# Transposing one batch entry's states ahead of the tokens and the other three behind the first probabilities

## The chip, the cores and the metric

One core of a Trainium2 chip runs the whole kernel. The metric is the device time of one execution in microseconds (us). The kernel before took 754.21 us (median of 3 runs, 754.07 to 754.38). The trace is of one further execution, the profiled one. Its engines: PE (TensorE), ACT (ScalarE), DVE (VectorE), POOL (GpSimd), SP (which here only issues DMAs).

## The reference, cut to what matters

```python
B, H, S, Ns, D = 4, 8, 512, 32, 64
scores  = x @ state.T / sqrt(D);  a  = softmax(scores)     # x reads the states
xread   = a @ state
scores2 = state @ x.T / sqrt(D);  a2 = softmax(scores2)    # the states read x
sread   = a2 @ x
t = concat([xread, sread], axis=2)          # (B, H, S + Ns, D) -> 2176 tokens x 512
t = elu(t @ w_in)   @ w_out                 # 512 -> 2048 -> 512, f64 weights in DRAM
t = mish(t @ w2_in) @ w2_out
```

## The kernel before, in words

Everything is float32; a product that needs full accuracy is split into high and low parts (three matmuls). The 16 slices of 128 hidden columns are one loop ("steps"); first-layer steps run over the four batch entries, second-layer steps over five blocks of tokens.

The part around the change is the head. For batch entry b and half hf of the heads, `token_reads` loads x (`xb`), turns it (`xT`, two turns of four 128x128 transposes, each evacuated by one copy), multiplies by the states (`scores`, 16 matmuls per half), takes the maximum over the 32 states (`mx`, L614), subtracts it (L615), exponentiates (L617), sums, inverts and multiplies (L621 to L624), turns the probabilities (`pT`, L629) and copies them to `x1` (L633). A copy of the raw scores (L618) goes to SBUF and then to DRAM (`s2d`), for the reads in the other direction much later. The states are kept as block-diagonal tiles `sd[b]`: `states()` loads all of them (`st_raw`, two DMAs on the ACT queue), transposes them in three groups of 2, 2 and 4 (entry 0; entry 1; entries 2 and 3; L388) and copies each half of `sd[b]` out of PSUM (8 copies, L394, shown under the helper's line L275). `xread @ w_in` is not formed: `fold` multiplies the states into the first weight (`m`, L516), so that the first step's matmul `h` (L721) is `m` against `x1`.

Weights come as 64-bit floats: each 512 KB tile is a DMA on the SP queue, one ACT conversion (`wy`, L439) and three DVE operations (L448, L450, L461 or L467).

The order of all instructions is computed at build time by `Plan`. Each operation has an engine (or `EITHER` of ACT and DVE), a cost and a due time, derived backwards from its successors or given. `run` (L117) repeatedly picks, over all engines, the operation with the smallest key

```python
k = (t, due, seq)      # t: the earliest start, by the planner's own clock
```

so the due time decides only between operations that could start at the same planned moment; an engine that is free takes whatever can start first. Buffers and PSUM banks are waited for as well. Early banks are dealt out in the fixed cycle of L342 in the order in which operations are added: in the kernel before entry 0's states and the second turn of half 1's x have the same bank, acc0. Afterwards every engine runs its own list strictly in that order, and semaphores guard what is read. Constants: raw-score copies are due at `T[index[1, b, 0]] - 8.0`, with `T` = 20.0 for the first step; x loads are due at -30, the warm-up turns at -40.

Of the kernel before, what the change touches and what calls it, by code (L numbers as in the profile page):

```python
# [22 lines left out]
P = 128  # L23
# [192 lines left out]
def attention_elu_mish(  # L216
# [49 lines left out]
    def buf(pool, tag, bufs, shape, dt=F32, name=None):  # L266
        return Buf(pool, tag, bufs, shape, dt, f"{name or tag}{next(serial)}")
# [103 lines left out]
        attention.append(op)  # L371
        return op

    def states():

        raw = buf("w", "w_out", NF, [P, 2 * B, 2, D], F32, "st_raw")
        for i in range(2):
            A(ACTQ, 128.0, lambda i=i: nc.scalar.dma_start(
                out=raw[:, :, i, :], in_=state.rearrange("b (g h) n d -> (h n) (b g) d", g=2)),
              w=[(raw, i)], due=-50.0)  # L380
        for b in range(B):
            A("POOL", 0.5, lambda b=b: nc.gpsimd.memset(sd[b], 0.0), w=[("sd", b, i) for i in range(2)], due=-50.0 + b)
        for b0, b1 in ((0, 1), (1, 2), (2, 4)):
            pt = bank("st")

            def turn(b0=b0, b1=b1, pt=pt):
                for i in range(2 * (b1 - b0)):
                    nc.tensor.transpose(pt[:, i * P:(i + 1) * P], raw[:, 2 * b0 + i].rearrange("p t d -> p (t d)"), ident)  # L388

            A("PE", 0.25 * (b1 - b0), turn, r=["ident", (raw, 0), (raw, 1)], w=[pt])  # L390
            for b in range(b0, b1):
                for i in range(2):
                    r = slice(i * D, (i + 1) * D)
                    A(EITHER, {"ACT": 0.41, "DVE": 0.43}, lambda e, b=b, b0=b0, i=i, r=r, pt=pt: copy(  # L394
                        e, sd[b][r, :, :, i, :],
                        pt[r, (b - b0) * 2 * P:(b - b0 + 1) * 2 * P].rearrange("p (g h n) -> p g h n", g=2, n=NS)),
                        r=[pt], w=[("sd", b, i)])
# [166 lines left out]
    def token_reads(b, hf):  # L564
        xb = load_x(b, hf, X_DUE if early else None)
        if b not in x1:
            if b:
                x1[b] = buf("work", "x", 2, [P, 2, 2, S], F32R, f"x1_{b}_")
            else:
                x1[b] = buf("w", "w_out", NF, [P, 2, S], F32, f"x1_{b}_")  # L570
        xt = x1[b]
        if early and hf:
            xT = buf("w", "w_out", NF, [P, 2, S], F32, "xT")
            prr = buf("w", "w_out", NF, [P, 2, NC, P], F32, "prob")
            pr, raw = (lambda: prr[:, 0]), (lambda: prr[:, 1])
            kp, kr = (prr, 0), (prr, 1)
            held = [prr]
        else:
            xT = buf("at", "xT", 1, [P, 2, S], F32)
            kp, kr = buf("at", "prob", 1, [P, NC, P], F32), buf("at", "raw", 1, [P, NC, P], F32)  # L580
            pr, raw = (lambda: kp.t), (lambda: kr.t)
            held = [kp, kr]
        mx = buf("at", "mx", 2, [P, NC * HH])
        sm = buf("at", "sm", 2, [P, NC * HH])
        held += [mx, sm]
        lag = 0.0 if early else 1.0
        ahead = TOKENS_AHEAD[b]
        for q in range(2):
            pt = bank("xT")

            def turn(q=q, pt=pt):
                for i in range(4):
                    nc.tensor.transpose(  # L593
                        pt[:, i * P:(i + 1) * P],
                        xb[:, 2 * q + i // 2, i % 2 * 2:i % 2 * 2 + 2, :].rearrange("p c d -> p (c d)"), ident)

            A("PE", NC * 0.11, turn, r=["ident", (xb, q)], w=[pt], lag=lag, place=[xT])
            A(EITHER, both(S), lambda e, q=q, pt=pt: copy(e, xT[:, q, :], pt.t), r=[pt], w=[(xT, q)])
        pt = bank("scores")
        for q in range(2):  # L600
            def score(q=q):
                for i in range(4):
                    h, c = 2 * q + i // 2, i % 2 * 2
                    nc.tensor.matmul(  # L604
                        pt.t.rearrange("p (c h n) -> p c h n", c=NC, n=NS)[:, c:c + 2, h, :],
                        lhsT=xT[:, q, i * P:(i + 1) * P], rhs=sd[b][:, hf, h, :, :], start=True, stop=True)

            A("PE", 0.9, score, r=[(xT, q), ("sd", b, 0), ("sd", b, 1)], w=[(pt, q)], lag=lag, place=held)
        all_c = [(pt, q) for q in range(2)]
        G = NC * HH  # L610
        prg = lambda: pr().rearrange("p c (h n) -> p (c h) n", n=NS)
        pv = lambda: pt.t.rearrange("p (g n) -> p g n", n=NS)
        wide = lambda t: t.t.unsqueeze(2).to_broadcast([P, G, NS])
        A("DVE", 0.69, lambda: nc.vector.tensor_reduce(mx.t, pv(), AX.X, ALU.max), r=all_c, w=[mx])  # L614
        A("DVE", 0.69, lambda: nc.vector.tensor_tensor(prg(), pv(), wide(mx), ALU.subtract),  # L615
          r=all_c + [mx], w=[kp])
        A("ACT", 0.64, lambda: nc.scalar.activation(pr(), pr(), AF.Exp, scale=SCALE), r=[kp], w=[kp], lag=lag)  # L617
        A(EITHER, both(S), lambda e: copy(e, raw().rearrange("p c f -> p (c f)"), pt.t), r=all_c, w=[kr],  # L618
          due=T[index[1, b, 0]] - 8.0)
        A(SP, 256.0, lambda: nc.sync.dma_start(out=s2d[:, b, hf], in_=raw()), r=[kr], w=[("s2d", b, hf)])  # L620
        A("DVE", 0.69, lambda: nc.vector.tensor_reduce(sm.t, prg(), AX.X, ALU.add), r=[kp], w=[sm])  # L621
        A("DVE", 0.17, lambda: nc.vector.tensor_scalar(sm.t, sm.t, EPS, None, ALU.add), r=[sm], w=[sm])
        A("DVE", 0.25, lambda: nc.vector.reciprocal(sm.t, sm.t), r=[sm], w=[sm])
        A("DVE", 0.69, lambda: nc.vector.tensor_tensor(prg(), prg(), wide(sm), ALU.mult), r=[kp, sm], w=[kp])  # L624
        p2 = bank("pT")

        def turn2():
            for c in range(NC):
                nc.tensor.transpose(p2[:, c * P:(c + 1) * P], pr()[:, c, :], ident)  # L629

        A("PE", NC * 0.11, turn2, r=["ident", kp], w=[p2], lag=lag, place=[xt])
        if not b:
            A(EITHER, both(S), lambda e: copy(e, xt[:, hf, :], p2.t), r=[p2], w=[(xt, hf)], lag=ahead)  # L633
        else:
            A(EITHER, both(S), lambda e: copy(e, xt[:, 0, hf, :], p2.t), r=[p2], w=[(xt, hf, 0)])
            A("DVE", 0.69, lambda: nc.vector.tensor_tensor(
                xt[:, 1, hf, :], p2.t, xt[:, 0, hf, :].bitcast(F32), ALU.subtract),
              r=[p2, (xt, hf, 0)], w=[(xt, hf)], lag=ahead)
# [184 lines left out]
    def retire(kind, blk, j, acc, s):  # L823
# [20 lines left out]
        t0, n = (NC * blk, NC) if kind == 1 else BLOCKS2[blk]  # L844
        second = kind == 1 and j == NF - 1 and (blk, 0, NF) not in FIRST
        for i, a in enumerate(acc):
            rows = x2d[:, i, t0 * P:t0 * P + S] if kind == 1 else None
            names = [("x2d", t0 + c, i) for c in range(NC)]
            if second:
                o = buf("work", "wraw", 3, [P, DM], F32, f"half{blk}_{i}_")  # L850
                add(SP, 256.0, lambda o=o, rows=rows: nc.sync.dma_start(out=o.t, in_=rows), r=names, w=[o], lag=2.0)
                add("DVE", 0.69, lambda o=o, a=a: nc.vector.tensor_tensor(o.t, a.t, o.t, ALU.add),
                    r=[a, o], w=[o], due=due + 0.7 * i)
            else:
                o = place(f"o{kind}_{blk}_{i}_")
                add(EITHER, both(S), lambda e, o=o, a=a: copy(e, o.t, a.t), r=[a], w=[o], due=due + 0.7 * i)
            if kind == 1:
                add(SP, 256.0, lambda o=o, rows=rows: nc.sync.dma_start(out=rows, in_=o.t), r=[o], w=names,
                    due=due + 4.0)
            elif t0 + i < NT - 1:  # L860
                b, c = divmod(t0 + i, NC)
                to = out[b * ST:b * ST + S, :].rearrange("(p c) e -> p c e", c=NC)[:, c, :]
                add(SP, 256.0, lambda o=o, to=to: nc.sync.dma_start(out=to, in_=o.t), r=[o], due=due + 4.0)
            else:
                add(SP, 256.0, lambda o=o: nc.sync.dma_start(
                    out=out.rearrange("(b s) e -> b s e", b=B)[:, S:, :], in_=o.t), r=[o], due=due + 4.0)
# [16 lines left out]


    warm()
    states()
    token_reads(0, 0)
    token_reads(0, 1)
    early = False
    s_state = index[0, 0, 0]  # L890
    for j in range(NF):
# [75 lines left out]
GATE_READS, GATE_READS_STEP, GATE_SECOND = 10, 4, 14  # L967
BACKLOG, RATE = 3.0, 330.0
OBUFS = 4
WHOLE_OUT = 6  # L970
X_WEIGHT = 1.5
POOL_LO = set()
# [28 lines left out]
```

## Time and profile before

| what | value |
| --- | --- |
| median of 3 runs | 754.21 us |
| the profiled execution's own time | 754.74 us |
| its span, first to last instruction | 752.8 us |
| PE busy | 732.8 us, 97% |
| DVE busy | 556.5 us, 74% |
| ACT busy | 423.3 us, 56% |
| mean DMA rate | 109 GB/s, 81.7 MB |

The span leaves 1.9 us around it in the profiled execution, which is 0.53 us longer than the median of the runs. Busy time is summed over instructions; PE's pipelined matmuls overlap a little.

### The profile page before, as it was taken

The page shows a single profiled execution, that of the slowest core. Times are in us where ns is not written, and L with a number is a line of the kernel's source. Part 1 is how long each engine was busy: PE and PEld are TensorE (multiplying, and loading weights), DVE is VectorE, ACT ScalarE, POOL GpSimd, SP SyncE. Part 2 cuts the span into 40 slices and gives each one's busy share as a digit, 9 for nine tenths or more (in the row PEclk, how much of TensorE's full clock was granted, in tenths as well). Part 3 has the DMA queues.
Part 4 walks back from the last instruction along what each step waited for, and adds up shares of the span by engine and source line. Part 5 has one row for each costly group of instructions (what it writes and reads, how often), then busy time and mean ns, then how long its engine had stood idle before and what let it go on. Part 6 is the DMA issues. An engine that isn't in the chain of part 4 may idle for free.

```text
span 752.8 us, 11041 instructions
## 1 busy us (share of the span) xinstructions
PE 732.8 (97%) x4098; PEld 597.8 (79%) x4098; DVE 556.5 (74%) x1047; ACT 423.3 (56%) x757; POOL 10.6 (1%) x27
## 2 busy tenths in 40 slices
PE   5899999999999999999999999999999999999995
PEld 5346677788787879878888888888889898989894
DVE  6989899988689895698998856565566666666653
ACT  3584767655566663487666545454455555455542
POOL 1000000010000000000000000000000000000000
PEclk9899999999999999999999999999999999999998
DMA  9954667363585643565855103000020020001001
GB/s 227 293 148 105 165 156 224 112 168 112 152 250 175 192 139 100 183 199 181 281 175 187 40 1 98 0 1 1 0 99 1 1 84 1 1 1 42 1 1 42
DMA packets 66872, 81.71 MB, mean 109 GB/s; under 512 B 22660, under 2 KB 45188, under 8 KB 66820
## 3 DMA queue, kind: packets, MB, share of 16 engines
q1 hardware_dynamic: 64740, 80.49, 36.0%
q10 hardware_dynamic: 2080, 0.52, 0.3%
q8 instruction: 32, 0.52, 0.3%
q14 instruction: 20, 0.16, 0.1%
HBM read 59.51 MB, written 21.50 MB: 108 GB/s over the span
## 4 chain that ended last, share of the span: by engine, by line
PE 94%; DMA 3%; DVE 1%; ACT 1%; issue 0%; SPq 0%; ACTq 0%
PE acc_acc L815 16%; PE acc_acc L817 15%; PE acc_acc L816 15%; PE h L735 12%; PE h L737 12%; PE h L736 12%; PE fold L516 2%; PE acc_acc L803 2%; PE h L711 2%; PE h L721 2%; DMA raw_in<-in_moe_w_in 2%; PE scores L604 1%; DMA xb<-in_x 1%; PE pT L629 1%; PE sr L663 1%; PE xT L593 1%
## 5 line engine op out<-in xcount | busy, mean ns | idle before, releaser
L754 ACT ACTIVATE e<-h 128x512 f32<-128x512 f32 (+1 forms) x148 | 83.1, 562 | 117.5 <-PE h L737 104.9
L779 ACT CAST g<-e 128x512 fp32r<-128x512 f32 (+1 forms) x142 | 82.4, 580 | 60.8 <-PE acc_acc L817 24.3
L737 PE MATMUL h<-x,w_in 128*128 128x384 f32 (+1 forms) x320 | 114.6, 358 | 0.0
L735 PE MATMUL h<-x,w_in 128*128 128x384 f32 (+1 forms) x320 | 114.4, 358 | 0.0
L736 PE MATMUL h<-x,w_in 128*128 128x384 f32 (+1 forms) x320 | 114.3, 357 | 0.0
L780 DVE TENSOR_TENSOR g<-e,g 128x512 fp32r<-128x512 f32 (+1 forms) x142 | 91.1, 642 | 22.3 <-ACT g L779 21.5
L817 PE MATMUL acc_acc<-w_out,g 128*128 128x512 f32 x272 | 106.9, 393 | 0.0
L816 PE MATMUL acc_acc<-w_out,g 128*128 128x512 f32 x272 | 106.7, 392 | 0.0
L815 PE MATMUL acc_acc<-w_out,g 128*128 128x512 f32 x272 | 105.9, 389 | 0.4 <-ACT g L779 0.4
L815 PE MATMUL acc_acc<-g,w_out 128*128 128x512 f32 x232 | 93.3, 402 | 0.0
L776 DVE TENSOR_TENSOR u<-u,e 128x384 f32<-128x384 f32 (+1 forms) x80 | 48.8, 610 | 57.8 <-ACT e L775 57.7
L817 PE MATMUL acc_acc<-g,w_out 128*128 128x512 f32 x232 | 90.5, 390 | 0.0
L816 PE MATMUL acc_acc<-g,w_out 128*128 128x512 f32 x232 | 90.5, 390 | 0.0
L774 ACT ACTIVATE e<-u,two 128x384 f32<-128x384 f32 (+1 forms) x80 | 52.8, 660 | 50.0 <-DVE u L772 49.8
L771 DVE TENSOR_SCALAR e<-e 128x384 f32<-128x384 f32 (+1 forms) x80 | 30.9, 387 | 48.2 <-ACT e L754 48.2
L735 PEld LDWEIGHTS h<-x,w_in 128*128 128x128 f32 x320 | 60.1, 188 | 7.2
L736 PEld LDWEIGHTS h<-x,w_in 128*128 128x128 f32 x320 | 60.1, 188 | 7.1
L737 PEld LDWEIGHTS h<-x,w_in 128*128 128x128 f32 x320 | 60.0, 188 | 4.9
L817 PEld LDWEIGHTS acc_acc<-w_out,g 128*128 128x128 f32 x272 | 51.0, 188 | 11.0 <-DVE g L780 0.3
L815 PEld LDWEIGHTS acc_acc<-w_out,g 128*128 128x128 f32 x272 | 51.1, 188 | 10.1 <-ACT g L779 0.9
L816 PEld LDWEIGHTS acc_acc<-w_out,g 128*128 128x128 f32 x272 | 51.0, 188 | 9.6
L815 PEld LDWEIGHTS acc_acc<-g,w_out 128*128 128x128 f32 x232 | 43.5, 188 | 13.5 <-issue 3.3
(126 smaller groups left out, 1168.9 us busy)
## 6 DMA issues: line engine op xcount, KB each, us to landing
raw_out<-in_moe_w_out SPq DMA_DIRECT2D x32, 512.0 KB, 3.9
raw_in<-in_moe_w_in SPq DMA_DIRECT2D x32, 256.0 KB, 5.9
raw_in<-in_moe_w_in SPq DMA_DIRECT2D x16, 512.0 KB, 4.3
w2d<-wv SPq DMA_DIRECT2D x32, 256.0 KB, 3.1
out<-o SPq DMA_DIRECT2D x17, 256.0 KB, 2.3
xb<-in_x SPq DMA_DIRECT2D x16, 256.0 KB, 4.6
x2d<-o SPq DMA_DIRECT2D x16, 256.0 KB, 2.6
xb<-in_x SPq DMA_DIRECT2D x32, 128.0 KB, 3.6
```

The costliest lines, as they stand in the source:

```text
L735: nc.tensor.matmul(h[:, :n], lhsT=wh, rhs=xh, start=(k == 0), stop=False)
L736: nc.tensor.matmul(h[:, :n], lhsT=wh, rhs=xl, start=False, stop=False)
L737: nc.tensor.matmul(h[:, :n], lhsT=wl, rhs=xh, start=False, stop=(k == nk - 1))
L754: add("ACT", act(n), lambda: nc.scalar.activation(E(), Hh(), AF.Exp), r=[h], w=[e])
L771: add("DVE", 0.1 + 0.00065 * n, lambda: nc.vector.tensor_scalar(E(), E(), E20, None, ALU.min), r=[e], w=[e])
L774: add("ACT", act(n) + 0.12, lambda: nc.scalar.activation(E(), U(), AF.Ln, bias=two), r=[u, "two"], w=[e])
L776: add("DVE", dve(n), lambda: nc.vector.tensor_tensor(U(), U(), E(), ALU.mult), r=[u, e], w=[u])
L779: add("ACT", act(n) + 0.01, lambda: nc.scalar.copy(g[:, 0, :n], E()), r=[e], w=[(g, 0)])
L780: add("DVE", dve(n), lambda: nc.vector.tensor_tensor(g[:, 1, :n], E(), g[:, 0, :n].bitcast(F32), ALU.subtract), r=[e, (g, 0)], w=[(g, 1)])
L815: nc.tensor.matmul(acc.t, lhsT=st[:, 0, :], rhs=mv[:, 0, :], start=fst, stop=False)
L816: nc.tensor.matmul(acc.t, lhsT=st[:, 0, :], rhs=mv[:, 1, :], start=False, stop=False)
L817: nc.tensor.matmul(acc.t, lhsT=st[:, 1, :], rhs=mv[:, 0, :], start=False, stop=lst)
```

## The change

Entry 0's transposes get a due time of -10. The other three entries' are added after both halves of entry 0's token reads and must come after the last copy of the probabilities to `x1` (`late_after`). The planner's cost of an early x turn goes from 0.44 to 0.84. Early copies of raw scores are due at 20 + 15 instead of 20 - 8. Because the operations are added in another order, early banks are dealt out differently: in the order entry 0's states, entry 0's x and scores, then the other states (att, acc1).

```diff
-    def states():
+    late_after, st_raw = [], []
+    def load_states():
         raw = buf("w", "w_out", NF, [P, 2 * B, 2, D], F32, "st_raw")
...
-        for b0, b1 in ((0, 1), (1, 2), (2, 4)):
+    def states(b0, b1):
...
-            A("PE", 0.25 * (b1 - b0), turn, r=["ident", (raw, 0), (raw, 1)], w=[pt])
+            op = A("PE", 0.25 * (b1 - b0), turn, r=["ident", (raw, 0), (raw, 1)], w=[pt], due=-10.0 if b0 == 0 and LATE else None,
+                   after=late_after if b0 and LATE else ())
...
-            A("PE", NC * 0.11, turn, r=["ident", (xb, q)], w=[pt], lag=lag, place=[xT])
+            A("PE", NC * (0.21 if early and LATE else 0.11), turn, r=["ident", (xb, q)], w=[pt], lag=lag, place=[xT])
...
-          due=T[index[1, b, 0]] - 8.0)
+          due=T[index[1, b, 0]] + (15.0 if early and LATE else -8.0))
...
-    states()
+    load_states()
+    states(0, 1)
+    if not LATE:
+        states(1, 2)
+        states(2, 4)
     token_reads(0, 0)
     token_reads(0, 1)
+    if LATE:
+        late_after.append(plan.writer[x1[0], 1])
+        states(1, 2)
+        states(2, 4)
...
+TILES_FROM = 4
+SPLIT_END = False
+LATE = True
```

The diff also adds two branches that these constants leave unused: scores by tiles for entries from `TILES_FROM` = 4 on (there are four, 0 to 3), and a last store in halves (`SPLIT_END` is False).

## Rows read from the trace of the kernel before

**Rows 1.** The page: the span, and two lines of the table of 40 equal slices (18.8 us each): PE's busy tenths and the share of the DMA engines.

```profile
span 752.8 us, 11041 instructions
PE   5899999999999999999999999999999999999995
DMA  9954667363585643565855103000020020001001
```

**Rows 2.** The chain that ended last, in order of time, of the first 28 us: start, us, what.

```profile
7.74 8.17 DMA raw_in<-in_moe_w_in
...
16.01 0.66 ACT wy L439
...
16.69 0.59 ACT prob L275
...
17.31 0.70 DVE mx L614
...
21.10 1.08 PE pT L629 x4
...
23.28 2.87 PE h L721 x4
```

**Rows 3.** Busy time by stretch: PE, PE's weight loads, DVE, ACT, POOL, then the granted TensorE clock (1.00 is 2.4 GHz), the share of the DMA engines and GB/s.

```profile
18.00:21.00 3.00, 0.68 (x14) 0.25 (x14) 2.90 (x7) 1.06 (x3) 0.00 (x0) 0.60 1.10 265
21.00:26.00 5.00, 4.89 (x12) 2.61 (x12) 4.75 (x10) 1.75 (x3) 0.00 (x0) 0.56 1.08 297
28.00:40.00 12.00, 12.00 (x70) 4.45 (x70) 10.76 (x20) 8.36 (x16) 0.00 (x0) 1.00 0.93 270
...
80.00:90.00 10.00, 8.57 (x52) 6.71 (x37) 8.54 (x18) 6.83 (x12) 0.00 (x0) 1.00 0.60 137
```

**Rows 4.** PE's instructions in order of time: start, us, line, output and inputs, count, and idle time before with what ended it.

```profile
6.29 3.25 PE L593 MATMUL xT<-ident,xb 128*128 128x128 f32 x16
...
11.69 3.76 PE L604 MATMUL scores<-sd,xT 128*128 128x64 f32 x32 [1.04 <-DVE sd L275]
...
18.87 0.68 PE L516 MATMUL fold<-w,sd 64*32 64x128 f32 x14 [3.09 <-DVE prob L615]
21.10 2.18 PE L629 MATMUL pT<-ident,prob 128*128 128x128 f32 x8 [1.55 <-DVE sm L622]
...
26.07 0.45 PE L516 MATMUL fold<-w,sd 64*32 64x128 f32 x16
27.07 0.74 PE L516 MATMUL fold<-w,sd 64*32 64x256 f32 x16 [0.56 <-ACT m L275]
27.74 1.98 PE L721 MATMUL h<-x,m 128*128 128x512 f32 x4
29.66 0.66 PE L516 MATMUL fold<-w,sd 64*32 64x256 f32 x16
```

**Rows 5.** ACT's instructions in order of time, the same columns.

```profile
11.30 0.66 ACT L439 ACTIVATE wy<-raw_in 128x512 f32<-128x512 f32 x1 [0.62 <-DMA raw_in<-in_moe_w_in]
...
13.61 0.67 ACT L439 ACTIVATE wy<-raw_in 128x512 f32<-128x512 f32 x1 [0.86 <-DMA raw_in<-in_moe_w_in]
...
16.01 0.66 ACT L439 ACTIVATE wy<-raw_in 128x512 f32<-128x512 f32 x1 [1.33 <-DMA raw_in<-in_moe_w_in]
16.69 0.59 ACT L275 COPY prob<-scores 128x512 f32<-128x512 f32 x1
17.17 0.63 ACT L617 ACTIVATE prob<-prob 128x512 f32<-128x512 f32 x1
...
26.67 0.43 ACT L275 COPY m<-fold 128x128 f32<-128x128 f32 x2
```

**Rows 6.** DVE's instructions in order of time, the same columns.

```profile
14.32 0.43 DVE L448 TENSOR_SCALAR wv<-wy 128x512 uint32<-128x512 uint32 x1 [0.44 <-ACT wy L439]
14.78 0.69 DVE L275 COPY raw<-scores 128x512 f32<-128x512 f32 x1
15.38 0.68 DVE L614 TENSOR_REDUCE mx<-scores 128x16 f32<-128x512 f32 x1
16.10 0.69 DVE L615 TENSOR_TENSOR prob<-scores,mx 128x512 f32<-128x512 f32 x1
17.31 0.69 DVE L614 TENSOR_REDUCE mx<-scores 128x16 f32<-128x512 f32 x1 [0.51 <-ACT prob L275]
...
21.97 0.68 DVE L450 SCALAR_TENSOR_TENSOR wv<-raw_in,wv 128x512 uint32<-128x512 uint32 x1
```

**Rows 7.** The states' tiles: line, engine, operation, count, then the shortest, median and longest duration in ns and the first and last start; the last row is the time from issue to landing of the two state loads.

```profile
L388 PE MATMUL st<-ident,st_raw x8: 272/273/328, 9.4 to 10.4; 128*128 128x128 f32 x8
L275 DVE COPY sd<-st x4: 416/417/428, 9.9 to 11.1; 64x256 f32<-64x256 f32 x4
L275 ACT COPY sd<-st x4: 366/367/368, 10.3 to 14.3; 64x256 f32<-64x256 f32 x4
L378 ACTq DMA_DIRECT2D st_raw<-in_state x2: 495/548/602, 0.8 to 1.3; - x2
DMA to landing us min/median/max: 4.3/5.1/5.9
```

**Rows 8.** Four probability transposes in the chain of waits, later, at the full clock: start, us, what.

```profile
75.14 0.44 PE pT L629 x4
```

**Rows 9.** What PE waited for after 60 us, up to 110 us: us in total, times, the longest.

```profile
PE h L735 <- DVE e L764: 1.4, 1, 1.4
```

More of the change, by code (lines that the diff above doesn't have):

```diff
@@ L382, in states @@
             A("POOL", 0.5, lambda b=b: nc.gpsimd.memset(sd[b], 0.0), w=[("sd", b, i) for i in range(2)], due=-50.0 + b)
-        for b0, b1 in ((0, 1), (1, 2), (2, 4)):
+        st_raw.append(raw)
+    def states(b0, b1):
+        raw = st_raw[0]
+        if True:
             pt = bank("st")
@@ L595, in turn, with score_tiles, turn_back @@
                         xb[:, 2 * q + i // 2, i % 2 * 2:i % 2 * 2 + 2, :].rearrange("p c d -> p (c d)"), ident)
-            A("PE", NC * 0.11, turn, r=["ident", (xb, q)], w=[pt], lag=lag, place=[xT])
+            A("PE", NC * (0.21 if early and LATE else 0.11), turn, r=["ident", (xb, q)], w=[pt], lag=lag, place=[xT])
             A(EITHER, both(S), lambda e, q=q, pt=pt: copy(e, xT[:, q, :], pt.t), r=[pt], w=[(xT, q)])
-        pt = bank("scores")
-        for q in range(2):
+        if b >= TILES_FROM:
+            ps = [bank("scoresT") for t in range(2)]
+            sTt = buf("at", "raw", 1, [P, NC, P], F32, "sT")
+            sT = lambda t: sTt[:, 2 * t:2 * t + 2, :]
+            def score_tiles():
+                for h in range(HH):
+                    for t in range(2):
+                        r, l = slice(t * D, (t + 1) * D), slice(h * NS, (h + 1) * NS)
+                        nc.tensor.matmul(ps[t][l, 0:2 * P], lhsT=sd[b][r, hf, h, t, :],
+                                         rhs=xT[r, h // 2, h % 2 * 2 * P:(h % 2 + 1) * 2 * P],
+                                         start=True, stop=True, tile_position=(t * D, h * NS))
+            A("PE", 0.7, score_tiles, r=[(xT, 0), (xT, 1), ("sd", b, 0), ("sd", b, 1)], w=ps, lag=lag, place=[sTt])
+            for t in range(2):
+                A(EITHER, both(2 * P), lambda e, t=t: copy(
+                    e, sT(t).rearrange("p c f -> p (c f)"), ps[t][:, 0:2 * P]), r=[ps[t]], w=[(sTt, t)])
+            pt = bank("scores")
+            for t in range(2):
+                def turn_back(t=t):
+                    for c in range(2):
+                        nc.tensor.transpose(pt[:, (2 * c + t) * P:(2 * c + t + 1) * P], sT(t)[:, c, :], ident)
+                A("PE", 0.25, turn_back, r=["ident", (sTt, t)], w=[(pt, t)], lag=lag,
+                  place=[i for i in held if i is not kr])
+        else:
+            pt = bank("scores")
+        for q in range(2 if b < TILES_FROM else 0):
             def score(q=q):
@@ L846, in retire @@
         for i, a in enumerate(acc):
+            if SPLIT_END and kind == 2 and blk == len(BLOCKS2) - 1:
+                o = place(f"o{kind}_{blk}_{i}_")
+                if t0 + i < NT - 1:
+                    b, c = divmod(t0 + i, NC)
+                    to = out[b * ST:b * ST + S, :].rearrange("(p c) e -> p c e", c=NC)[:, c, :]
+                else:
+                    to = out.rearrange("(b s) e -> b s e", b=B)[:, S:, :]
+                for hf, e in enumerate(EITHER):
+                    r = slice(hf * DM // 2, (hf + 1) * DM // 2)
+                    add(e, both(DM // 2)[e], lambda o=o, a=a, r=r, e=e: copy(e, o[:, r], a[:, r]), r=[a], w=[(o, hf)],
+                        due=due + 0.7 * i)
+                    q, eng = ((ACTQ, nc.scalar), (SP, nc.sync))[hf]
+                    if i < n - 1:
+                        q, eng = SP, nc.sync
+                    add(q, 128.0, lambda o=o, to=to, r=r, eng=eng: eng.dma_start(
+                        out=to[..., r], in_=o[:, r]), r=[(o, hf)], due=due + 4.0)
+                continue
             rows = x2d[:, i, t0 * P:t0 * P + S] if kind == 1 else None
```

## The prediction, made before the result was known

> **What bounds the kernel now.** I read the page's slices first. PE is full from the third slice to the last but one; only the first two, 37.6 us, and the last leave it idle, and in the first two the DMA engines are busy for nine tenths [rows 1]. The change touches only the head, so the question is when PE becomes full and whether it stays so. The table by stretch answers: at 28 to 40 us PE is busy for 12.00 of 12 us, and after that the only wait worth a name is 1.4 us near 82 us, on a DVE operation [rows 3, 9]. A microsecond gained before 26 us is kept if PE doesn't lose it again; a microsecond of PE work put behind 26 us is paid in full.
>
> What sets the 26 us? The chain of waits [rows 2]: the third weight tile lands (7.74 + 8.17 = 15.91 us), ACT converts it (16.01), ACT copies half 1's raw scores (16.69), DVE takes half 1's maximum (17.31), and the softmax runs to the probabilities' transposes at 21.10 and to `h` at 23.28. The scores themselves are not on it. They start at 11.69, after 1.04 us of waiting for a state copy, and end at 11.69 + 3.76 = 15.45 [rows 4]; half 0's 16 matmuls are half of that, so they are done near 13.6, yet its maximum starts at 15.38, because DVE was first held by the second weight (wait of 0.44 for `wy`, L448 at 14.32) and then by the raw copy at 14.78 [rows 6].
>
> **The change, part by part.** I follow the planner by hand from its costs in the code; its clock gives an order of instructions, never a time here.
>
> *Entry 0 first.* Its two transposes are now the first turn behind the warm-up and its two copies come before all others. On the chip they must wait for the state loads: the second is issued near 1.3 and lands at most 5.9 later, near 7.2 [rows 7], where x's turns started at 6.29 [rows 4]. So about 0.9 us is lost, x's turns take their 3.25 again, and the scores begin near 10.5 to 11 instead of 11.69 and, at 3.76, end near 14.5. That is an estimate, and it matters little: what follows them is not waiting for them, and with the wait on the loads twice as long they would still end at 15.4.
>
> *The raw copies.* The new due time is meant to let them go later. But the key is the earliest start first. In the planner's clock the warm-up ends at 5.35, the states at 5.60, four x turns at 0.84 each at 8.96, and the scores' four groups at 0.9 each at 9.86, 10.76, 11.66 and 12.56. ACT has ended the second weight at 10.41 and has nothing else it could start, so it takes half 0's raw copy at 10.91, the moment it is ready; DVE, which took the second weight's L448 at 10.82, comes to the maximum at 11.25. Half 1's raw copy can start at 12.71, its rival on ACT, half 0's exponential, at 12.78. So both copies stay where they were, ahead of the exponentials, and due times never decide. On ACT the order is: second weight, raw 0, third weight, raw 1, exponential 0.
>
> With the rows' durations: raw 0 moves from DVE to ACT and runs behind the second weight, 14.3 to 14.9 [rows 5]; half 0's maximum goes at about 14.93 instead of 15.38, its subtraction ends near 16.3, and DVE fills the time to 17.0 with the second weight's L450 (0.68, at 21.97 before) [rows 6]. Then half 1's maximum: raw 1 still stands on ACT behind the third weight, which lands at 15.91, and ends at 17.28 [rows 5]. In the trace the maximum waited 0.51 for that copy though it doesn't read it [rows 6]; both read one bank. So it starts at 17.31 again, and everything to 21.10 is as before: term 0. Its bounds: -1.2 (raw 0's 0.60 on DVE, and the 0.51 wait, both gone) and +0.5 (one more operation of DVE's, 0.4 to 0.7, ahead of it).
>
> The Trainium skill's page "PSUM — Partial Sum Buffer", section "PSUM bank collisions raise a hardware error", says that no two engines may be at one bank at once, reads against reads included, so software puts them in order; the 0.51 above agrees. By that rule a raw copy that is planned first on another engine always holds the maximum, and the term stays 0; only if it were planned last would it be -1.2.
>
> *Six transposes behind the probabilities.* They leave a place where PE waited anyway (9.4 to 10.7) and come after `h`, when PE is full. At the full clock four such transposes take 0.44 [rows 8], so six take 0.66: +0.65. Bounds: 0 (they fall in a gap) and +1.3 (the 0.27 of one alone, with 0.05 more between two, times four [rows 7]).
>
> *The gap before the second step.* Before, PE stood 0.56 at 26.5 waiting for ACT's copies of `m` (two at 26.67), since the fold was behind the first `h` [rows 4, 5]. The second weight's L450 and L461 are now done earlier, so in the planner's order this fold slips between the two halves of `h`, and the copies run beside it: -0.56.
>
> *Folds of entry 1 that no longer fill.* They need `sd[1]`, which now comes late. Before, two of them (0.74 at 27.07 and 0.66 at 29.66) kept PE busy while ACT and DVE made the next `m` [rows 4]. Now PE reaches the third step's `h` with those copies perhaps not made: between 0 and 0.9 (ACT's two copies at 0.43 behind one weight conversion), I take 0.4.
>
> *Six copies in a stretch without air.* At 28 to 40 DVE is busy for 10.76 of 12 and ACT for 8.36 [rows 3]; six copies at 0.42 or 0.37 [rows 7] come into it. PE has the work of two steps in hand, so they are hidden at first; what they can reach is the 1.4 us wait at 82 [rows 9]. None of it: 0; three copies on DVE: 1.26; all six: 2.5. ACT has the spare time, so I take 0.2. Two of them hold the accumulator's bank acc1 until done; the planner then takes the other accumulators first.
>
> DMA: no transfer is added. The loads keep their order, since they wait for buffers that don't change; the two `s2d` stores were late before and stay behind the loads.
>
> Sum: 0 + 0.65 - 0.56 + 0.4 + 0.2 = +0.7. The profiled execution took 754.74 (its span of 752.8 and 1.9 around it, which I leave as it is), so 755.4; it was 0.53 above the median of the runs, so 754.9 there.
>
> **The clock.** It is at 0.60 for 18 to 21 and 0.56 for 21 to 26, against 1.00 at 28 to 40 [rows 3], so at the level of 1.2 GHz for most of that time, and PE had idled for 3.09 us before 18.87 [rows 4]; the probabilities' transposes took 2.18 for eight, where full clock gives 0.88 [rows 4, 8], and `h` 2.87 where the next took 1.98. So 1.3 and about 0.9, in all 2.2 us, is what the lower level costs. The scores' earlier end only lengthens the idle time, and PE's return at 21.10 is the same, so I leave this out of the sum.
>
> **Rivals.**
>
> *A, faster: the maxima run free of the raw copies.* If ACT's copies stand behind the exponentials, the softmax starts 1.2 earlier, and with the gap closed the sum is -1.2 + 0.65 - 0.56 = -1.1, or 753.1. If the shorter idle time also keeps the clock up, another 2.2 comes off: 750.9. For it: the copies are in the chain [rows 2], and margins in my planning by hand are as small as 0.07. Against: an idle ACT takes what starts first.
>
> *B, slower: the moved copies reach the full DVE.* Place: the wait on DVE at 82 us, which is there already [rows 9]. Price: 0.42 per copy that goes to DVE in 24 to 80 us and isn't made up, with the transposes 0.65 and the missing folds 0.9, less the 0.56. With three copies that is 0.65 + 0.9 + 1.26 - 0.56 = +2.3 or 756.5; with six +3.5 or 757.7. It decides the sign beyond 0.2% from two copies on. For it: DVE works at nine tenths from 28 us on. Against: 3.6 us of ACT's 12 are free there.
>
> *C: nothing moves on the path at all,* neither gap nor folds: 0.65 for the transposes, 754.9 as well. It is within my forecast.
>
> **How the numbers follow.** 0.2% of 754.21 is 1.5 us, about what a measurement of this kernel tells from none: faster is below 752.7, slower above 755.7. Forecast with C 0.41, its own range 753.0 to 755.7; A 0.33; B 0.26. The range reaches from the middle of A's two prices (751.9) to between B's (757.0), which leaves about one in ten out on each side.
>
> **What would show it.** Right: entry 0's transposes ahead of x's, the raw copies on ACT ahead of both maxima, half 1's maximum at 17.3, `pT` at 21.1, no gap at 26.5, six transposes after 24 us. Wrong: `pT` before 20.5 (A), the wait near 82 us above 2.5 (B), another landing time of the third weight, or PE's clock at 1.00 through 18 to 26 us. The order beyond 30 us I haven't followed; a new wait of PE anywhere there would break the sum.

## The result and the profile after

The changed kernel took 763.51 us (median of 4 runs, 763.06 to 764.41) against 754.30 for the kernel before (4 runs): ratio 1.0116, 95% interval [1.0104, 1.0128]. It is 1.2% slower, 8.6 us above the forecast and 6.5 above the end of the range. The profiled execution took 763.86 with a span of 761.9; before it was 754.74 and 752.8 [rows 1].

The page of the kernel after: busy time by engine, then PE's and the clock's slices (19.0 us each).

```profile
span 761.9 us, 11037 instructions
PE 735.7 (97%) x4098; PEld 600.5 (79%) x4098; DVE 557.8 (73%) x1044; ACT 425.7 (56%) x760; POOL 10.6 (1%) x27
PE   5699999999999999999999999999999999999995
PEclk9699999999999999999999999999999999999999
```

PE was busy 732.8 us before and is 735.7 now: of the 9.1 us that the span has grown, PE is busy for 2.9 and idle for 6.2. Only the second slice shows it (6 where [rows 1] has 8). The table by stretch says where. First the kernel before, then after; columns as in [rows 3].

```profile
18.00:26.00 8.00, 5.57 (x26) 2.86 (x26) 7.65 (x16) 2.82 (x6) 0.00 (x0) 0.57 1.09 285
26.00:33.00 7.00, 6.45 (x73) 2.31 (x72) 5.77 (x11) 5.87 (x12) 0.00 (x0) 1.00 1.09 306
33.00:40.00 7.00, 7.00 (x44) 2.87 (x31) 6.11 (x12) 4.32 (x9) 0.00 (x0) 1.00 0.83 227
40.00:62.00 22.00, 21.91 (x90) 11.07 (x89) 18.69 (x35) 17.06 (x32) 0.00 (x0) 1.00 0.58 156
```

```profile
18.00:26.00 8.00, 5.71 (x42) 2.89 (x43) 7.53 (x17) 2.69 (x7) 0.00 (x0) 0.57 1.09 283
26.00:33.00 7.00, 2.81 (x12) 1.35 (x11) 4.05 (x8) 3.53 (x6) 0.00 (x0) 0.93 1.08 303
33.00:40.00 7.00, 6.32 (x29) 3.10 (x30) 2.46 (x5) 3.53 (x8) 0.00 (x0) 0.58 0.81 245
40.00:62.00 22.00, 20.27 (x93) 9.83 (x91) 19.95 (x36) 15.47 (x29) 0.00 (x0) 1.00 0.46 130
```

Up to 26 us nothing is lost. Then PE is idle for 4.19 of 7 us, for 0.68 of the next 7, in which its clock is also at 0.58, and for 1.73 of the 22 after that. PE's instructions in order of time name the places:

```profile
7.18 0.66 PE L394 MATMUL st<-ident,st_raw 128*128 128x128 f32 x2 [0.68 <-DMA st_raw<-in_state]
11.04 3.92 PE L638 MATMUL scores<-sd,xT 128*128 128x64 f32 x32
...
20.96 2.18 PE L663 MATMUL pT<-ident,prob 128*128 128x128 f32 x8 [1.55 <-DVE sm L656]
22.93 1.92 PE L755 MATMUL h<-x,m 128*128 128x512 f32 x2
24.78 0.60 PE L523 MATMUL fold<-w,sd 64*32 64x128 f32 x16
25.32 2.84 PE L755 MATMUL h<-x,m 128*128 128x512 f32 x6
27.99 0.82 PE L394 MATMUL st<-ident,st_raw 128*128 128x128 f32 x6
33.01 1.09 PE L600 MATMUL xT<-ident,xb 128*128 128x128 f32 x4 [4.20 <-DMA xb<-in_x]
34.77 1.12 PE L600 MATMUL xT<-ident,xb 128*128 128x128 f32 x4 [0.68 <-ACT xT L275]
35.68 3.46 PE L837 MATMUL acc_acc<-gw,whole 128*128 128x512 f32 x4
...
58.27 0.66 PE L600 MATMUL xT<-ident,xb 128*128 128x128 f32 x4 [0.72 <-ACT xT L275]
59.23 1.03 PE L523 MATMUL fold<-w,sd 64*32 64x256 f32 x16 [0.31 <-DVE prob L649]
60.96 1.07 PE L523 MATMUL fold<-w,sd 64*32 64x256 f32 x16 [0.70 <-ACT m L275]
```

Down to 28.8 us this is the forecast, line by line. Then comes an instruction that the kernel before has at 53.85: the turn of batch entry 1's x. PE's list holds it at 28.8, its data land at 32.9, and PE runs its list in order. The four `acc_acc` matmuls behind it (the first step's hidden values against its output weight, `whole`) take 3.46 us; four of them took 1.98 in the kernel before, at 33.28. The other engines' lists have the same hole. ACT's, then DVE's, in order of time:

```profile
34.13 0.59 ACT L275 COPY xT<-xT 128x512 f32<-128x512 f32 x1 [4.09 <-PE xT L600]
34.62 0.67 ACT L446 ACTIVATE wy<-raw_in 128x512 f32<-128x512 f32 x1
```

```profile
35.31 0.43 DVE L455 TENSOR_SCALAR wv<-wy 128x512 uint32<-128x512 uint32 x1 [3.91 <-ACT wy L446]
```

One early turn stops three engines: ACT stands at its copy, with a weight conversion (L446) next in its list, and DVE waits for that weight.

**Why the turn is there.** I followed the planner on, past where my working had stopped. By its clock (an order, not a time) it is at 24.47 when PE has done `h` of the first two steps and the late state turns. It has nothing else for PE: folds of entry 1 want `sd[1]`, which now comes late, and the next fold of entry 0 wants both `att` banks, one of which the late states of entry 1 hold until their copies are made. Entry 1's x is planned to have landed at 24.3, so its turn is free to start and takes the other `att` bank, which that entry's scores then keep; folds of entry 0 slip, one to a planned 48.58. The planner counts loads at 330 KB per us (`RATE`, line 1027). The DMA view of the kernel after, by fortieths of the first 45 us:

```profile
GB/s 0 28 258 288 293 258 349 223 219 219 216 215 215 214 219 240 371 220 216 218 234 300 408 354 202 239 321 360 342 370 390 262 143 153 324 0 0 0 0 0
```

and the chain of waits (start, us, what):

```profile
22.22 10.65 DMA xb<-in_x
...
33.01 1.10 PE xT L600 x4
```

From 8 to 18 us the queues moved 214 to 240 GB/s, and so entry 1's x landed 8.6 us later than planned.

### The profile page after: what moved, and what is told of

The parts are those of the page before. It is cut to its first block, busy times and chain, and to the rows that moved or that the text cites. A ratio compares the mean times of both kernels' runs of the same rounds, so it can differ in the third digit from the quotient of the medians.

```text
span 761.9 us, 11037 instructions
## 1 busy us (share of the span) xinstructions
PE 735.7 (97%) x4098; PEld 600.5 (79%) x4098; DVE 557.8 (73%) x1044; ACT 425.7 (56%) x760; POOL 10.6 (1%) x27
## 4 chain that ended last, share of the span: by engine, by line
PE 93%; DMA 4%; ACT 1%; DVE 1%; SPq 0%; issue 0%; ACTq 0%
PE acc_acc L849 15%; PE acc_acc L851 15%; PE acc_acc L850 15%; PE h L769 12%; PE h L771 12%; PE h L770 12%; PE acc_acc L837 3%; DMA raw_in<-in_moe_w_in 2%; PE fold L523 2%; PE h L745 2%; PE h L755 1%; DMA xb<-in_x 1%; PE scores L638 1%; PE xT L600 1%; PE sr L697 1%; PE acc_att L849 0%
```

## The experiments

Theory T: PE's list holds entry 1's x turn before its data have landed, and the loss is that wait, the clock that falls in it, and the banks and lists behind it. Several kernels need an earliest planned start for an operation; they share this helper, and then give `nb=` to the operations named:

```diff
-    def add(self, engs, cost, fn, r=(), w=(), due=None, lag=0.0, after=(), place=()):
+    def add(self, engs, cost, fn, r=(), w=(), due=None, lag=0.0, after=(), place=(), nb=0.0):
...
-            t = 0.0
+            t = op.nb
```

**The turn held back.** The kernel after, with entry 1's x turns not before the planner's 34.

```diff
-            A("PE", NC * (0.21 if early and LATE else 0.11), turn, r=["ident", (xb, q)], w=[pt], lag=lag, place=[xT])
+            A("PE", NC * (0.21 if early and LATE else 0.11), turn, r=["ident", (xb, q)], w=[pt], lag=lag, place=[xT],
+              nb=34.0 if b == 1 else 0.0)
```

> The change as it is, but the planner may not start entry 1's x turns before its own 34 (on the chip their x lands near 33; the planner had them at 24.5). Theory T (the loss is PE's in-order wait for entry 1's x, and what follows it: the lower clock and the folds that come late because the turn and its scores hold the bank): no PE wait on a DMA after 26 us, PE clock 1.00 from 26 us on, 754 to 757 us. Rival R (the moved transposes and copies themselves, in a stretch where DVE is full): still 761 or more, with PE waits on DVE or ACT in place of the wait on the DMA.

Measured: 755.23 (10 runs, 754.58 to 756.3), ratio 1.0005 [0.9995, 1.0015]. Of the loss of 1.16%, 1.11% is gone, 8.4 us with some 1.2 of uncertainty: T. PE's waits from 24 to 120 us in this kernel (us in total, times, longest):

```profile
PE acc_acc L838 <- DVE whole L474: 1.6, 1, 1.6
PE h L770 <- DVE e L799: 0.8, 1, 0.8
```

No load is waited for. What is left is everything else the change does, and it can't be told from no change.

**The clock alone.** The kernel after, with 38 transposes of the identity ahead of the waiting turn, into the tile that the turn then overwrites: the wait stays, but PE is busy in it.

```diff
+                if b == 1 and not hf and not q:
+                    turns(pt, 38)
```

> The change as it is, with 38 transposes of the identity ahead of entry 1's first x turn, into the same bank, which the turn overwrites: PE is busy while it waits. Prices the clock alone. T: x lands at 33 as before, so the 4.2 us stay, but the clock stays at 1.00 through 33 to 39 us, where PE was busy about 5 us at half speed: 2 to 3 us less than the change, 760.5 to 761.5. If the clock has no part: 763.5 as the change.

Measured: 761.49 (4 runs), ratio 1.0090 [1.0075, 1.0105], 0.26% below the kernel after: 2.0 us, give or take 1.4. By stretch, and PE in order of time:

```profile
26.00:33.00 7.00, 7.00 (x50) 5.61 (x48) 4.22 (x8) 3.63 (x7) 0.00 (x0) 1.00 1.08 293
33.00:39.00 6.00, 4.92 (x35) 2.46 (x34) 3.38 (x7) 4.46 (x10) 0.00 (x0) 1.00 0.92 283
```

```profile
28.79 4.31 PE L351 MATMUL xT<-ident 128*128 128x128 f32 x38
33.51 0.66 PE L602 MATMUL xT<-ident,xb 128*128 128x128 f32 x4 [0.41 <-DMA xb<-in_x]
...
35.33 1.88 PE L839 MATMUL acc_acc<-gw,whole 128*128 128x512 f32 x4
```

The granted clock is 1.00 to 39 us and the four `acc_acc` take 1.88 instead of 3.46. So it is the idle wait that brings the clock down to 1.2 GHz (0.50 in each microsecond from 33 to 38 in the kernel after), and that is worth about a quarter of the loss; the turn still starts at 33.5. The profiled execution is the slowest of the four (763.24; the others took 761.12 to 761.53). Its second fold of 64x256 behind 56 us starts at 59.04, in the kernel after at 60.96, so by then 1.92 us are gained, which agrees with the 2.0. Of these it has lost 1.6 by 65 us, since its clock is at 0.50 a second time, from 60 to 62 us, behind the three waits of 56 to 59 us; in the kernel after the row stays at 1.00 behind the same waits.

**Banks and what they push back.** The kernel after, with entry 1's scores held back: the turn stays early and the wait with it, but the scores no longer hold the banks.

```diff
-            A("PE", 0.9, score, r=[(xT, q), ("sd", b, 0), ("sd", b, 1)], w=[(pt, q)], lag=lag, place=held)
+            A("PE", 0.9, score, r=[(xT, q), ("sd", b, 0), ("sd", b, 1)], w=[(pt, q)], lag=lag, place=held,
+              nb=45.0 if b == 1 else 0.0)
```

> The change as it is, entry 1's x turns early as in it, but its scores may not start before the planner's 45, so they can't hold one of the two banks that the folds of entry 0 need. Prices the second part of the loss, the three PE waits of 1.7 us in all at 58 to 61 us. T: the wait of about 4 us on x and the lower clock stay, the waits at 58 to 61 go: 761 to 762.2. If the banks have no part: 763.5.

Measured: 760.71 (4 runs), ratio 1.0078 [1.0065, 1.0091], 2.9 us below the kernel after, give or take 1.3. PE's waits from 24 to 120 us (the one left out is 0.2):

```profile
PE xT L600 <- DMA xb<-in_x: 3.8, 1, 3.8
PE xT L600 <- ACT xT L275: 0.7, 1, 0.7
PE h L770 <- DVE e L799: 0.6, 1, 0.6
...
```

The three waits of 58 to 61 us (1.73 together) are gone, and the one on `e` is 0.6 where the kernel after has 1.4. I had expected 1.7, and 761 us at the least; these two make 2.5. Why the wait on `e` is shorter here wasn't tried.

**The planner's rate.** The kernel after with a plan that counts loads as slower.

```diff
-BACKLOG, RATE = 3.0, 330.0
+BACKLOG, RATE = 3.0, 240.0
```

> The change as it is with one constant of the planner altered: the load rate that it assumes, 240 instead of 330 KB per us (the trace moves 215 to 290 GB/s in the head). The planner then expects entry 1's x later and, by its rules, puts the turn at its 50 instead of 24.5. T (a wrong landing time in the plan is the cause): no PE wait on a DMA after 26 us, 754 to 757. Rival R (the moved work costs by itself): 760 or more.

Measured: 757.25 (9 runs), ratio 1.0043 [1.0029, 1.0057]. At 240 KB per us the planner itself has entry 1's x land at 32.5 (32.9 in the trace of the kernel after) and turns it at 50.27. No wait for a load after 19 us, as T has it, but not the time of the first experiment, and just above the 757 that I gave T. The runs fall into two groups, 756.2 to 757.3 (five) and 759.5 to 760.1 (four), and the profile is one of the upper, with scores of 6.93 us instead of 3.92 (last section). Its order differs too: half 1's probabilities are turned only behind the first `h` at 24.18. The rate alters many decisions at once, so this bears T out on the wait and on nothing else.

**Without the edge to the probabilities.** The kernel after, in which the other three entries' states may be turned once their data are there.

```diff
-        late_after.append(plan.writer[x1[0], 1])
```

> The change without the rule that the other states come after the probabilities (entry 0 first, due times and turn costs as in the change). The planner's order, worked out from its rules, still has an x turn of entry 1 early, at its 24.5, now behind the third step's fold. T: PE waits for x near 28 to 33 us again and the time is 757 to 763. Rival S (it is the other states' lateness that costs): 754 to 755.5.

Measured: 759.93 (4 runs), ratio 1.0069 [1.0053, 1.0084]. PE, in order of time:

```profile
18.55 0.75 PE L523 MATMUL fold<-w,sd 64*32 64x128 f32 x16 [1.76 <-ACT sd L275]
...
32.90 0.63 PE L600 MATMUL xT<-ident,xb 128*128 128x128 f32 x4 [2.95 <-DMA xb<-in_x]
```

The states are early again and the turn is early still, with 2.95 us of waiting. It isn't the lateness of the states by itself that costs.

**The due time alone.** The kernel before, with only the early raw copies due at 20 + 15.

```diff
-          due=T[index[1, b, 0]] - 8.0)
+          due=T[index[1, b, 0]] + (15.0 if early else -8.0))
```

> The kernel before with one edit, the due time of the early raw copies (20 + 15 instead of 20 - 8); nothing else of the change. T: the planner's order now has entry 1's first x turn at its 26.2, ahead of the first accumulations, so PE waits for x until about 33 us though no state was moved: 757 to 762. Rival (only the moved states matter, and due times decide nothing): 754 to 755.

Measured: 758.46 (4 runs), ratio 1.0047 [1.0032, 1.0062].

```profile
29.24 1.09 PE L516 MATMUL fold<-w,sd 64*32 64x256 f32 x32
32.94 1.09 PE L593 MATMUL xT<-ident,xb 128*128 128x128 f32 x4 [2.61 <-DMA xb<-in_x]
```

A due time that I had said decides nothing is enough, in the kernel before, to bring the same turn to the same place and to lose 0.47%. The two folds right ahead of it (29.24) are entry 1's by the planner's order: here they do fill, and the turn comes early all the same.

**The raw copies held back as well.** The first experiment's kernel, with the two early raw copies behind the planner's 16, which is what rival A describes.

```diff
-          due=T[index[1, b, 0]] + (15.0 if early and LATE else -8.0))
+          due=T[index[1, b, 0]] + (15.0 if early and LATE else -8.0), nb=16.0 if early else 0.0)
```

> As the run with entry 1's turns late, and the early raw copies may not start before the planner's 16, so that they really stand behind both exponentials. Prices rival A of the prediction (-1.2 from the softmax). T: half 1's maximum near 16.1 instead of 17.2, pT near 19.9 instead of 21.2, and the time 0.5 to 1.2 below the run with the turns late: 754.0 to 754.7. If something else holds the softmax as late (the exponential behind the third weight, DVE's own work): pT near 21 and 755.2.

Measured: 754.73 (11 runs) against 754.97 for before (26 runs), ratio 1.0001 [0.9992, 1.0009]. DVE, then ACT, then PE, in order of time:

```profile
16.66 0.69 DVE L649 TENSOR_REDUCE mx<-scores 128x16 f32<-128x512 f32 x1
```

```profile
19.11 0.59 ACT L275 COPY prob<-scores 128x512 f32<-128x512 f32 x1
```

```profile
19.75 0.67 PE L523 MATMUL fold<-w,sd 64*32 64x128 f32 x14 [3.81 <-DVE sm L656]
...
22.36 2.04 PE L756 MATMUL h<-x,m 128*128 128x512 f32 x2
```

Half 1's maximum starts at 16.66 instead of 17.44 (the first experiment), so the copy's hold on it is gone. But now the copies end at 19.70 and the first fold starts at 19.75; it stands ahead of the transposes in PE's list, and I take it to wait for the bank that the copies read. The chain is 0.84 us shorter at `h` (22.36 for 23.20), and the runs don't resolve a gain.

**Weights' conversions held back too.** The first experiment's kernel with the raw copies at `nb=14.88`, due at 15, and four of ACT's weight conversions behind them.

```diff
-            r=[raw], w=[y])
+            r=[raw], w=[y], nb={("in", 1): 14.9, ("in", 2): 16.0, ("in", 3): 18.5, ("out", 0): 20.5}.get((kind, j), 0.0) if layer == 1 else 0.0)
```

> As the run with the raw copies behind, and the ACT conversions of the second to fourth first-layer weights and of the first second-layer one may not start before the planner's 14.9, 16, 18.5 and 20.5, so the exponentials don't stand behind a load that hasn't landed; the raw copies may go from 14.88 on, with a due time of 15. T: the landing of the second and third weights (13.5 and 15.9) no longer sets the softmax; half 0's maximum near 13.7, pT near 19.5, 753.0 to 754.5, below the kernel before. Rival: the softmax is bound by DVE's own work or the scores' end, pT near 21, no gain.

Measured: 755.16 (median of 11 runs, 754.39 to 758.48 but for one of 1891.72), ratio 1.0006 [0.9995, 1.0017]. No gain. Half 0's maximum starts at 14.79, not at the 13.7 that I had expected: DVE has the first weight's three operations to do ahead of it, from 12.99 on. Half 0's transposes start at 20.61, but half 1's stand behind the first `h`, at 24.25.

**The states in the idle gap.** The kernel after without the edge to the probabilities, with entry 1's x turns and the raw copies held back as above; beside it, the kernel before with these two held back. The edits of both together (the `nb` values stand in each; the kernel before keeps its own due time and turn cost beside them):

```diff
-        late_after.append(plan.writer[x1[0], 1])
...
+              nb=34.0 if b == 1 else 0.0)
...
+          due=T[index[1, b, 0]] + (15.0 if early and LATE else -8.0), nb=16.0 if early else 0.0)
```

> The changed kernel without the edge that ties the states of entries 1 to 3 to the probabilities, with entry 1's x turns not before the planner's 34 and the two early raw copies not before its 16. Theory (the loss is the early x turn; what the version with late turns kept is 1.58 us of waiting on `whole`, because no fold of entry 1 fills it, and 0.66 us of turns in full PE): the six state turns fall into the idle time between the scores and the first fold, folds of entry 1 fill again, no wait for xb after 20 us, no wait on DVE `whole` above 0.5; 753.0 to 754.3, that is 0.998 to 1.000 of before. Rival (the loss of the late turns' version isn't the missing folds; the copies of the states hold DVE and ACT, and the banks, just when the softmax needs them): half 1's probabilities' transposes later than 21.5 and 754.7 to 756.

> The kernel before with the raw copies of entry 0 held behind the planner's 16 and entry 1's x turns not before its 34; states as before. Rival A of the prediction on its own (the maxima free of the raw copies are worth 1.2): half 1's maximum near 16.7, its transposes near 20, 753.0 to 753.4 (0.9985). Theory from the version with both held back (the first fold or the second half's transposes wait for the bank that the raw copies hold): transposes of half 0 earlier, the last of `h` no more than 0.5 earlier, 753.7 to 754.6, not to be told from before. If the x turns held back cost something of their own, above 755.

Measured: the first 753.88 (11 runs, 752.86 to 755.45) against 754.96 (21 runs), ratio 0.9985 [0.9976, 0.9994]; the second 754.44, ratio 0.9994 [0.9985, 1.0002]. PE in the first:

```profile
14.30 0.82 PE L394 MATMUL st<-ident,st_raw 128*128 128x128 f32 x6
20.02 1.09 PE L664 MATMUL pT<-ident,prob 128*128 128x128 f32 x4 [4.90 <-DVE prob L659]
...
27.46 1.09 PE L523 MATMUL fold<-w,sd 64*32 64x256 f32 x32
29.77 1.98 PE L838 MATMUL acc_acc<-gw,whole 128*128 128x512 f32 x4 [1.21 <-DVE whole L474]
```

The six turns cost nothing where PE has no work, and two folds stand at 27.46 where the first experiment's kernel has the six turns. Two points of the expectation missed: the wait on `whole` is 1.21, not under 0.5, and half 1's transposes come at 21.75, as the rival said. Still it is the only version whose interval lies wholly below the kernel before: by 1.1 us, which the interval puts between 0.5 and 1.8 and which is no more than the 0.2% that I said a measurement can tell. The second shows that a version of the kernel before gains nothing certain from late raw copies.

## Why the prediction was wrong, point by point

**The step that failed** is the sentence "The order beyond 30 us I haven't followed": by it the sum counts the planner's order behind the six transposes as unchanged, a term of nothing for which I gave no reason. The place is that of "*Folds of entry 1 that no longer fill*", with its price of 0 to 0.9. I asked what PE would lack there and priced the hole as a short wait on ACT's copies. I didn't ask what the planner would put into it. It put in entry 1's x turn, 21 us earlier than before on the chip, the wait included (33.01 for 53.85), and as the list is strict, a hole of 1.58 us (what is left of it with the turn held back) became a stop for a load. The missing folds aren't needed to draw the turn forward: with the due time alone two folds of entry 1 stand ahead of it, and it is early all the same. So the due time is enough for it by itself; whether another part of the change is too, no run isolates. I had also misread the banks: I wrote that two of the six copies hold acc1, but by the code four do, and the other two hold an `att` bank, the one that the next fold of entry 0 lacks.

The measured parts: the two waits at the turns, 4.20 + 0.68, less the 1.58 that the first experiment has on `whole` in that place, make 3.3; the clock 2.0; the banks 2.9. Together 8.2, beside 8.4 for holding the turn back. The parts were taken in different kernels, and the last two carry more than 1 us of uncertainty each, so the sum is a check of size and no more.

**The term of the folds, in its own terms, was too small as well.** With the turn held back, the hole is there as I described it: 1.58 us, not 0.4 and above my 0.9, and what ends last is DVE's output weight `whole`, not ACT's copies of `m`.

**Head, term 0: right.** Entry 0's states at 7.18 (forecast 7.2), scores from 11.04 to 14.96 (14.5 forecast, with no effect), raw copies on ACT ahead of the exponentials, half 1's maximum at 17.17 (17.3) after 0.44 of waiting for the copy, `pT` at 20.96 (21.1). The maximum, on DVE:

```profile
17.17 0.69 DVE L648 TENSOR_REDUCE mx<-scores 128x16 f32<-128x512 f32 x1 [0.44 <-ACT prob L275]
```

My argument for it was half right: the copies do stay, because they start first, but "due times never decide" was true of the two copies and not of the kernel (the due time alone: +0.47%).

**Six transposes, +0.65: right**, 0.82 measured at 27.99. **Gap at 26.5, -0.56: right**, the fold runs at 24.78 between the halves of `h` and no wait is left there. **Clock to 26 us: right**, 0.57 in both kernels.

**Six copies in a full DVE, +0.2 and rival B: not there.** The wait on `e` [rows 9], near 82 us before and 91 after, is 1.4 in both, and 0.8 with the turn held back; why it shrinks there wasn't tried. B had the sign, with another place, price and mechanism.

**Rival A: its mechanism is possible, not its price.** It didn't occur. Made to occur, it gave 0.84 us at `h`, not 1.2, where the wait for the bank seems to move to the fold, and no gain that the runs resolve.

**The sum without the failed step** was close: the first experiment is the change as I had described it, forecast +0.7 and measured +0.4 [-0.4, +1.1]. In part that is luck: the hole was 1.2 us larger than its term, while the wait on `e` became 0.6 shorter where I had added 0.2. Two small slips in the sums bear on nothing here: 0.60 and 0.51 make 1.1, not A's 1.2, and the ends of the range, by the prices it is taken from, are 752.0 and 757.1.

The test that I named ("a new wait of PE anywhere there would break the sum") was the right one. I gave it no chance and no price in the range.

## What to carry to other kernels

Where a planner fills holes, an edit that moves work out of a place must be followed until each engine's list agrees with the old one again; for each operation that comes earlier, set its data's landing in the trace (here 32.9) against the plan's (24.3). A strict list can turn a small hole into a stop on every engine that has a consumer in it: here a hole of 1.58 us became 4.20 us of PE's time, with ACT and DVE idle nearly as long (4.09 and 3.91), and PE's stop was paid again behind it, about 2.0 us, in matmuls at 1.2 GHz. When a change frees a resource in such a plan, bound what is drawn forward as well as the hole it fills: hold it back by an earliest start and see whether the time returns.

## What the runs showed of the hardware that I had not expected

The clock's row of a profile can say 1.00 where PE runs at half speed, because nothing was recorded there. The same 32 score matmuls at 11 to 18 us (line, form, count, busy us, mean ns, then the stretch), first in the kernel after, then in the one with the slower planned rate:

```profile
L638 PE MATMUL scores<-sd,xT 128*128 128x64 f32 x32 | 3.9, 284 | 0.0
...
11.00:18.00 7.00, 4.30 (x36) 3.96 (x34) 5.14 (x10) 4.06 (x7) 0.13 (x1) 1.00 1.14 219
```

```profile
L638 PE MATMUL scores<-sd,xT 128*128 128x64 f32 x32 | 6.9, 418 | 0.0
...
11.00:18.00 7.00, 7.00 (x35) 6.88 (x34) 3.92 (x7) 1.83 (x3) 0.13 (x1) 1.00 1.14 225
```

Both stretches show 1.00, yet one instruction takes 418 ns where the other takes 284, and x's turns ahead of them took 421 in both. The two levels can be told from the kernel before with late raw copies, whose 32 scores took 5.49 us: its scores take 277 ns at 12 to 13.5 us, where its row is at 1.00, and 421 at 14.5 to 17.5, where it is at 0.50. So 418 is the lower level. The traces say why the row misses it: the first clock record of the kernel after is at 11.5 us, that of the slower planned rate only at 30.2, and the view counts what has no record as 1.00. At the start of a kernel, then, the duration of a known instruction tells the level; the row does so only from the first record on. When PE comes up to speed differs between executions of the same head (11.5 and 30.2 us here). The Trainium skill's page "TensorE: Matmul & The Clock Gate", section "Seeing it yourself", warns that the clock events of a profile have been seen to be unreliable; here they are missing for the first 30.2 us. Four of nine runs some 3 us apart from the others fit an execution that comes up late, as the scores took 3.0 us more, though only one of them was profiled.
